# First pairs' loads and transposes rearranged, a written-out end, and the last chunk's rows as two halves, in a top-k attention and gated layer kernel

## The chip, the cores and the metric

The kernel runs on one core of one Trainium2 chip. The metric is the device time of that core in microseconds (us); of several executions the median counts.

## The reference

```python
scores = scale * np.matmul(q, k.transpose(0, 1, 3, 2))          # (8, 8, 576, 576), head size 64
kth = np.partition(scores, -32, axis=-1)[..., -32:-31]
scores = np.where(scores >= kth, scores, -1e9)
attn = softmax(scores)                                           # sum + 1e-09 below
x = np.matmul(attn, v).transpose(0, 2, 1, 3).reshape(4608, 512)
H = np.maximum(x @ w_h, 0.0)
T = 1.0 / (1.0 + np.exp(-(x @ w_t + b_t)))
out = T * H + (1.0 - T) * x
```

Each row of 576 scores keeps its 32 largest, goes through a softmax and is multiplied with v; the 4608 rows of 512 then pass a gated layer with two 512 x 512 weights.

## The kernel before, in words

**Tiling.** Of the 576 query rows of a head, four chunks have 128 rows and the last has 64. A unit is one full chunk of one head, or the last chunk of two heads (64 rows each, so 128 partitions). Two units make a pair; a batch has 18 pairs (four for each full chunk, two for the last chunk) and the run has 144, numbered 0 to 143. k and q are loaded with rows on partitions (`kin`, `qin`, one buffer each) and turned by TensorE (PE) into `kT` and `qT` by `prep_piece` (L210): part 0 turns k of a head pair, part 1 q, part 2 the 64 end rows of all heads.

**A step.** `step(i)` (L641) works on several pairs at once. For pair i+2 PE computes the scores (`start_scores`, L590); for pair i+1 VectorE (DVE) takes twelve MAX8 over segments of the scores in PSUM (`segs`, L603, with the MAX8 at L319), refines them to a threshold (`refine`, L324), ScalarE (ACT) copies the scores to SBUF (L314) and makes the masks (`masks_of`, L636); for pair i PE adds the masks into PSUM (`mask_add`, L373), DVE takes two MAX8 over 576 columns (`below`, L385), ACT takes the exponentials (L382) and the k-th value is picked (`hits`, `pick_a`, `pick_b`); for pair i-1 DVE masks the exponentials (`keep`, L428, or `keep_min` and `keep_mul`), and SyncE (SP) issues a DMA transpose (L447); for pair i-3 PE multiplies with v (`values`, L450) and ACT copies the sums out when four heads are in the bank (`back_xs`, L622). `spare(n)` (L240) issues n matmuls whose result is not used; their moving operand is the weight `wh`.

**The gated layer.** When a chunk's eight heads are there, `ffn_pieces` (L479) makes its pieces: `norm`, `xt` (PE turns x), `hh` and `tt` (the two products, through one PSUM bank, `fps`), each in a step of its own; their sums and products are single operations in the list `pool_work`, which GpSimd (POOL) works off, and the last of them stores the rows. The last chunk goes through this with 64 partitions and 512 columns.

**Start.** POOL sets the constants (L90 to L150), then issues the ten loads of v and the two of the weights (L174 to L203); SP issues the twenty loads of k and q of batch 0 (L158, L164). The code at L735 to L743 then does pair 0 by hand; `ensure_prep` (L575) turns the head pair that a score needs and has ACT copy it, one piece after the other, through the one `fps` bank.

**End.** L744 runs `step` three times more than there are pairs, so the last three steps hold only what is left; then a count over all thresholds makes a flag (L752 to L767), and L770 to L778 works off the rest of the gated layer, one piece at a time, with DVE in POOL's place. The flag decides whether a general second pass runs (L781); it does not run here.

The order on each engine is the order of this code (`manual_schedule`, L734).

Of the kernel before, what the change touches and what calls it, by code (L numbers as in the profile page):

```python
# [26 lines left out]
def kernel(  # L27
# [50 lines left out]
    xpool = ctx.enter_context(tc.tile_pool(name="x", bufs=2))  # L78
# [9 lines left out]
    nc.vector.tensor_copy(ident_b[:], ident_f[:])  # L88
    cst = consts.tile([P, P], BF16)
    nc.gpsimd.memset(cst[:], 1.0 / float(P))  # L90
    ones = consts.tile([P, 1], FP32)
    nc.gpsimd.memset(ones[:], 1.0)
    NPK = TOP_K - RANK + 1
    pidx = consts.tile([P, NPK], FP32)
    for jj in range(NPK):
        nc.gpsimd.memset(pidx[:, jj : jj + 1], S - 2.0 * (TOP_K - jj))
# [3 lines left out]
    nc.gpsimd.memset(fac[:, 0:2], -scale)  # L100
    nc.gpsimd.memset(fac[:, 2:4], -BIGK * (1.0 - 2.0**-24))
# [4 lines left out]
    for i in range(NE):  # L106
        en = consts.tile([P, 2, 2, 16], FP32, name=f"en{i}")
        nc.gpsimd.memset(en[:, 0, :, 0:1], 3.0e38)
        ends.append(en)
# [18 lines left out]
    for i in range(NM):  # L128
        m1 = consts.tile([P, S], BF16, name=f"m{i}")
        nc.gpsimd.memset(m1[:], 0.0)  # L130
        masks.append(m1)

    vbs = []
    for i in range(2):
        vb = consts.tile([P, H, nck, DE], BF16, name=f"vb{i}")
        nc.gpsimd.memset(vb[:], 1.0)
        vbs.append(vb)
    NEP = 4
    eps_sb = []
    for i in range(NEP):  # L140
        ep = consts.tile([P, SP], BF16, name=f"ep{i}")
        pad = S if i % 2 == 0 else 0
        nc.gpsimd.memset(ep[:, pad : pad + SP - S], 0.0)
# [10 lines left out]
    def loads_kq(b, kin, qin):  # L154
        both = ((k, kin), (q, qin))

        def head(src, dst, h):
            nc.sync.dma_start(  # L158
# [4 lines left out]
        def ends(src, dst, i):  # L163
            nc.sync.dma_start(  # L164
                dst[0:rem, :, J, i, :], src[b, i:H:2, J * P : S, :].rearrange("h p d -> p h d")
            )
# [26 lines left out]
    for load in loads_kq(0, kin, qin):  # L193
# [6 lines left out]
    for load in loads_v(0, vbs[0]):  # L200
        load()
    nc.gpsimd.dma_start(wh[:], moe_w_h.rearrange("(g p) n -> p g n", p=P))
    nc.gpsimd.dma_start(wt[:], moe_w_t.rearrange("(g p) n -> p g n", p=P))  # L203
    nc.scalar.dma_start(
        bt32[:], bass.AP(tensor=moe_b_t.tensor, offset=moe_b_t.offset, ap=[[0, P], [1, dm]])
    )
    nc.gpsimd.tensor_scalar_mul(bt[:], bt32[:], 0.5)


    def prep_piece(stage, prep, hp, part):  # L210
# [6 lines left out]
        ps = fps.tile([P, 512], FP32, tag="fp", name="fp")  # L217
        if part < 2:
# [3 lines left out]
            return lambda: nc.scalar.copy(dst[:, hp, 0 : nfull * P], ps[:, 0 : nfull * P])  # L222
# [7 lines left out]
        view = ps[:].rearrange("p (i h n) -> p i h n", i=2, n=rem)  # L230

        def evac():
            nc.scalar.copy(kd[0:D, :, 0:rem], view[0:D, 0, :, :])
            nc.scalar.copy(kd[D:P, :, rem : 2 * rem], view[D:P, 0, :, :])
# [5 lines left out]
    def spare(n):  # L240
        if "t" not in po:
            po.update(t=pso_tile(), n=0)
        for _ in range(n):
# [3 lines left out]
                wh[:, 0, 0 : BANK - 4 * DE],  # L247
# [201 lines left out]

    def values(pair, ets, vb, pso, col):  # L450
        for s, u in enumerate(pair):
            b, qt, heads = units[u]
            ql = rem if qt == nfull else P
            for gi, h in enumerate(heads):
                for c in range(nck):
                    vc = (c - s) % nck
                    nc.tensor.matmul(  # L457
                        pso[0:ql, col : col + DE],
# [11 lines left out]
    def xs_copy(qt, h0, n, pso, xs):  # L470
        ql = rem if qt == nfull else P
        nc.scalar.copy(xs[0:ql, h0 * DE : h0 * DE + n], pso[0:ql, 0:n])  # L472
# [5 lines left out]

    def ffn_pieces(b, qt, xs):  # L479
        ql = rem if qt == nfull else P  # L480
        st = {}

        def norm():
            xs3 = xs[0:ql, :].rearrange("p (h e) -> p h e", e=DE)
            rinv = cpool.tile([P, H], FP32, name="rinv")
            nc.vector.tensor_scalar(rinv[0:ql, :], xs3[:, :, D], 1e-9, 2.0, ALU.add, ALU.mult)
            nc.vector.reciprocal(rinv[0:ql, :], rinv[0:ql, :])
# [3 lines left out]
            def scaled(e):  # L491
                e.tensor_tensor(
                    x[0:ql, :].rearrange("p (h d) -> p h d", h=H),
                    xs3[:, :, 0:D],
                    rinv[0:ql, :].unsqueeze(2).to_broadcast([ql, H, D]),
# [6 lines left out]
        def xt():  # L502
            ps = fps.tile([P, 512], FP32, tag="fp", name="fp")
            for g in range(n_g):
                nc.tensor.transpose(
                    ps[:, g * P : g * P + ql], st["x"][0:ql, g * P : (g + 1) * P], ident_f[0:ql, 0:ql]
                )
# [3 lines left out]
            return lambda: nc.scalar.copy(xT[:, :, 0:ql], psv[:, :, 0:ql])  # L511

        def hh():
            ps = fps.tile([P, 512], FP32, tag="fp", name="fp")
            for g in range(n_g):
                nc.tensor.matmul(
                    ps[0:ql, :], st["xT"][:, g, 0:ql], wh[:, g, :], start=(g == 0), stop=(g == n_g - 1)
                )
# [5 lines left out]
            def evac():  # L524
                nc.scalar.activation(h2[0:ql, :], ps[0:ql, :], AF.Relu)
                pool_work.append(lambda e: e.tensor_add(s1[0:ql, :], h2[0:ql, :], x[0:ql, :]))
                pool_work.append(lambda e: e.tensor_sub(h2[0:ql, :], h2[0:ql, :], x[0:ql, :]))
# [3 lines left out]
        def tt():  # L531
            ps = fps.tile([P, 512], FP32, tag="fp", name="fp")
            for g in range(n_g):
                nc.tensor.matmul(  # L534
                    ps[0:ql, :], st["xT"][:, g, 0:ql], wt[:, g, :], start=(g == 0), stop=False
                )
            nc.tensor.matmul(ps[0:ql, :], cst[:, 0:ql], bt[:], start=False, stop=True)
# [3 lines left out]
            def last(e):  # L541
                o = fpool.tile([P, dm], FP32, name="o")
                e.tensor_add(o[0:ql, :], s1[0:ql, :], h2[0:ql, :])
                r0, r1, rs = (qt, J * P, J) if qt < nfull else (J * P, S, 1)
                if isinstance(b, int):
                    dst = out3[b, r0:r1:rs, :]
                else:
# [319 lines left out]
```

## Time and profile before

| | us |
|---|---|
| median of 3 runs | 855.37 (854.66 to 858.37) |
| profiled execution | 860.02 |
| its span, first to last instruction | 858.4 |
| DVE busy | 808.2 (94%) |
| ACT busy | 777.6 (91%) |
| PE busy | 728.8 (85%) |
| POOL busy | 522.2 (61%) |

Busy time is the time in which an engine executes an instruction; PE's is modelled, since matmuls overlap. [...] A line of the timeline tells its start, its length, the engine, the line of the code, what it wrote and read, how many alike follow each other, and in brackets how long the engine had been idle and whom it waited for.

### The profile page before, as it was taken

Reading aid. Unit: us, or ns where it says so; the run is one execution under the profiler, and the core shown is the slowest. Engines: PE = TensorE matmul, PEld = TensorE weight load, DVE = VectorE, ACT = ScalarE, POOL = GpSimd, SP = SyncE. Lnnn points to the kernel's source line nnn. Section 1 sums busy time; section 2 is a strip of 40 time slices with the busy share of each in tenths; the row PEclk is TensorE's granted clock in tenths of the full one; section 3 lists DMA queues with packets and bytes.
Section 4 is the critical chain, followed back from the end, with each engine's and each line's share of the span. In section 5 each row is a group of like instructions: output and inputs, shape, how many; then the busy total and the mean of one; then the engine's idle time right before and its main releaser. Section 6 shows DMA issues by size and latency. Waiting matters only on the chain.

```text
span 858.4 us, 20956 instructions
## 1 busy us (share of the span) xinstructions
PE 728.8 (85%) x6548; PEld 525.1 (61%) x6644; DVE 808.2 (94%) x4131; ACT 777.6 (91%) x1441; POOL 522.2 (61%) x690
## 2 busy tenths in 40 slices
PE   4788988889888888899888998888888998888874
PEld 3566766666566666566666665666665666665652
DVE  5599999999999999999999999999999999999973
ACT  3589998999999999999999999999999999999961
POOL 9145655766657566666656666576666666555560
PEclk9699999999999999999999999999999999999997
DMA  9466545666367545664555754576445644442331
GB/s 158 72 105 110 95 67 115 118 117 91 73 110 132 98 81 94 115 125 85 78 110 121 123 88 76 105 134 101 81 92 116 124 82 82 80 86 62 81 75 35
DMA packets 318631, 83.52 MB, mean 97 GB/s; under 512 B 312752, under 2 KB 313776, under 8 KB 318512
## 3 DMA queue, kind: packets, MB, share of 16 engines
q1 hardware_dynamic: 275072, 75.55, 42.9%
q0 software_dynamic: 43296, 6.30, 10.6%
q8 instruction: 54, 0.88, 0.4%
q14 instruction: 65, 0.53, 0.2%
q10 hardware_dynamic: 144, 0.26, 0.2%
HBM read 31.72 MB, written 9.44 MB: 48 GB/s over the span
## 4 chain that ended last, share of the span: by engine, by line
ACT 38%; PE 32%; DVE 25%; POOL 2%; issue 2%; DMA 1%; ACTq 0%; POOLq 0%; DVEq 0%
ACT m L363 10%; DVE wall L386 9%; DVE cand L319 9%; ACT e L382 9%; PE pso L244 8%; ACT sc L314 6%; PE xs L275 6%; ACT r L409 4%; PE xs L292 3%; PE pso L457 3%; PE fp L534 3%; PE xs L376 3%; ACT xs L472 2%; PE xs L284 2%; ACT kT L222 2%
## 5 line engine op out<-in xcount | busy, mean ns | idle before, releaser
L319 DVE MAX8 cand<-xs 128x8 f32<-128x96 f32 x1728 | 297.0, 247 | 22.2 <-PE xs L284 16.9
L244 PE MATMUL pso<-wh,ident_b 128*128 128x252 bf16 x1962 | 261.2, 273 | 47.7 <-ACT xs L472 45.5
L244 PEld LDWEIGHTS <-ident_b 128*128 128x128 bf16 x1962 | 186.5, 98 | 91.1 <-issue 59.6
L382 ACT ACTIVATE e<-sc,be 128x576 bf16<-128x576 f32 x288 | 228.2, 793 | 0.2 <-POOL be L357 0.2
L386 DVE MAX8 wall<-xs 128x8 f32<-128x576 f32 x288 | 203.8, 749 | 7.7 <-PE xs L376 4.2
L275 PE MATMUL xs<-kT,qT 64*128 64x256 f32 x1024 | 148.6, 406 | 37.8 <-DVE high L333 30.8
L314 ACT COPY sc<-xs 128x1152 f32<-128x1152 f32 x144 | 161.6, 1122 | 10.1 <-DVE cand L319 10.1
L420 POOL TENSOR_SCALAR ro<-sc,tk 128x576 bf16<-128x576 f32 x93 | 160.0, 1721 | 0.0
L275 PEld LDWEIGHTS xs<-kT,qT 64*128 64x128 f32 x1024 | 94.8, 189 | 67.5 <-issue 34.8
L402 POOL TENSOR_TENSOR hit<-hit,wall 128x18 f32<-128x18 f32 x144 | 32.6, 226 | 151.0 <-DVE hit L392 139.1
L363 ACT ACTIVATE m<-xs,wall 128x576 int8<-128x576 f32 x144 | 107.8, 749 | 15.9 <-DVE wall L349 15.7
L357 POOL TENSOR_TENSOR be<-tk,fac 128x4 f32<-128x4 f32 x145 | 28.8, 198 | 150.9 <-DVE ep L426 48.8
L409 ACT ACTIVATE r<-sc,be 128x576 bf16<-128x576 f32 x144 | 112.2, 779 | 1.9 <-POOL be L357 1.9
L363 ACT ACTIVATE m<-sc,wall 128x576 int8<-128x576 f32 x144 | 112.8, 783 | 0.0
L376 PE MATMUL xs<-m,ident_b 128*128 128x64 bf16 (+1 forms) x520 | 94.3, 277 | 10.6 <-ACT m L363 8.8
L457 PEld LDWEIGHTS <-et 128*128 128x128 bf16 (+1 forms) x1600 | 68.6, 100 | 18.9 <-issue 3.7
L457 PE MATMUL pso<-vb,et 128*128 128x65 bf16 (+1 forms) x1600 | 74.4, 194 | 3.6
L376 PEld LDWEIGHTS <-ident_b 128*128 128x128 bf16 x576 | 51.8, 98 | 38.7 <-issue 14.6
L284 PEld LDWEIGHTS xs<-kd,qT 128*128 128x128 f32 x256 | 38.7, 190 | 43.4 <-issue 43.4
L416 DVE TENSOR_TENSOR ep<-e,r 128x576 bf16<-128x576 bf16 x144 | 65.1, 452 | 0.0
L284 PE MATMUL xs<-kd,qT 128*128 128x128 f32 x256 | 63.4, 330 | 0.0
L174 POOL DMA_DIRECT2D vb<-in_v_dram x64 | 52.1, 815 | 7.1 <-issue 7.0
(87 smaller groups left out, 1184.0 us busy)
## 6 DMA issues: line engine op xcount, KB each, us to landing
kin<-in_k_dram SPq DMA_DIRECT2D x64, 128.0 KB, 2.6
qin<-in_q_dram SPq DMA_DIRECT2D x64, 128.0 KB, 3.1
out_dram<-o SPq DMA_DIRECT2D x32, 256.0 KB, 2.4
vb<-in_v_dram POOLq DMA_DIRECT2D x80, 64.0 KB, 3.1
et<-ep SPq DMA_TRANSPOSE x288, 2.5
kin<-in_k_dram SPq DMA_DIRECT2D x16, 64.0 KB, 2.5
qin<-in_q_dram SPq DMA_DIRECT2D x16, 64.0 KB, 2.4
out_dram<-o SPq DMA_DIRECT2D x8, 128.0 KB, 2.3
```

The source lines that it names most:

```text
L244: nc.tensor.matmul(po["t"][:, 4 * DE : BANK], ident_b[:], wh[:, 0, 0 : BANK - 4 * DE], start=True, stop=True, skip_group_check=True,)
L275: nc.tensor.matmul(ps[:, mo + n0 : mo + n0 + 256], qT[r : r + D, hp, qs : qs + P], kT[r : r + D, hp, n0 : n0 + 256], start=(n0 == 0), stop ...
L284: nc.tensor.matmul(ends, qT[:, hp, qs : qs + P], kd[:, hp, :], start=True, stop=True)
L314: nc.scalar.copy(sc[:], both)
L319: nc.vector.max(cand[:, s, :], sc[:, s * SEG : (s + 1) * SEG])
L363: nc.scalar.activation(m1[:].bitcast(I8)[:, 1 : 2 * S : 2], ps, AF.Sign, bias=wall[:, u, 0:1], scale=ABOVE, accum_out=csum[:, u : u + 1],)
L376: nc.tensor.matmul(ps[:, s0:s1], ident_b[:], m1[:, s0:s1], start=False, stop=True, skip_group_check=True)
L382: nc.scalar.activation(e[:], sc, AF.Exp, bias=tb(u), scale=scale)
L386: nc.vector.max(wall[:, u, 1:NPK], ps)
L409: nc.scalar.activation(r[:], sc, AF.Relu, bias=eb(u), scale=BIGK)
L420: nc.gpsimd.tensor_scalar(r[:], sc, kth(u), None, ALU.is_ge)
L457: nc.tensor.matmul(pso[0:ql, col : col + DE], ets[s][:, c, gi * P2 : gi * P2 + ql], vb[:, h, vc, :], start=(c == 0), stop=(c == nck - 1),)
```

## The change

Three parts. **Start:** the constants that POOL set go to DVE for the most part; both identities are made by POOL; of `vb` only the column of ones is set. The first q loads are issued by ACT, those of k by SP, the bias by SP at the end. The loads of v and of the weights (in four halves) come out of the start and are issued by POOL in steps 0 to 8, two in each of the steps 0 to 4, then one. `begin()` takes the place of the code at L735: 24 spare matmuls first, with the constant `cst` as moving operand in place of `wh`; then the three pieces of head pair 0 into three PSUM tiles, evacuated by ACT and DVE; the pieces of head pairs 1 and 2 go out ahead of their scores, and pair 3's in steps 0 and 1. **Last chunk as two halves:** its sums of heads 0 to 3 go to partitions 0 to 63, those of heads 4 to 7 to partitions 64 to 127, in one bank with one copy; the gated layer works on 128 partitions and 256 columns, with two groups of matmuls for each product and two stores. **End:** the loop stops after step 142, and `finish()` writes the rest out: all masks by the one-instruction form `keep` on DVE, the last pair's exponentials turned by PE instead of by DMA, the layer's three last blocks (z, ya, yb) in several PSUM banks with fused DVE operations (`blk_diff`, `blk_out`), and the count for the flag last.

```diff
-    nc.vector.tensor_copy(ident_b[:], ident_f[:])
+    make_identity(nc, ident_b[:])
-        nc.gpsimd.memset(vb[:], 1.0)
+        nc.gpsimd.memset(vb[:, :, :, D:DE], 1.0)
-    for load in loads_kq(0, kin, qin):
+    first, later = (loads_kq(0, kin, qin, eng) for eng in (nc.scalar, nc.sync))
+    early = first[0:12] + later[12:]
+    for load in early[0:8]:
         load()
-    for load in loads_v(0, vbs[0]):
-        load()
...
-                wh[:, 0, 0 : BANK - 4 * DE],
+                cst[:, 0 : BANK - 4 * DE],
...
+    def project(ps, qt, xT, w, bias):
...
+        nh, ng, wd = shape_of(qt)
+        for c in range(2):
+            o = ps[c * P2 : (c + 1) * P2, 0:wd]
+            cols = slice(c * wd, (c + 1) * wd)
+            for g in range(n_g):
+                r = g // ng * P2
+                nc.tensor.matmul(
+                    o, xT[:, g % ng, r : r + P2], w[:, g, cols], start=(g == 0), stop=(g == n_g - 1 and not bias)
+                )
...
-        if todo_v and k_in % 3 != 0:
+        for _ in range(min(len(todo_v), 2 if i < 5 else i <= SPB or k_in % 3 != 0)):
             todo_v.pop(0)()
+        if i == 4:
+            nc.gpsimd.tensor_scalar_mul(bt[:], bt32[:], 0.5)
...
+    def begin():
...
+        spare(24)
+        evs = [
+            piece(0, 0),
+            piece(0, 1, po["t"], dve),
+            piece(0, 2, xps.tile([P, 3 * BANK], FP32, tag="x", name="xs"), dve),
+        ]
+        po.clear()
+        for ev in evs:
+            ev()
         start_scores(0)
+        evs = [piece(1, 0), piece(1, 1, pso_tile())]
+        for ev in evs:
+            ev()
         segs(0, 2 * NSEG)
         copy_both(0)
         start_scores(1)
...
+        evs = [piece(2, 0), piece(2, 1, pso_tile())]
         masks_of(0)
+        for ev in evs:
+            ev()
+        to_prep.extend(((0, 3, 0), (0, 3, 1)))
...
+    def finish():
...
+        z = blocks[-1]
+        values_of(i - 3, 0)
+        for s in range(2):
+            mask_add(cur["ps"][s], cur["m"][s], s)
+        late.pop(0)()
+        zh = fps.tile([P, 512], FP32, tag="fp", name="fp")
+        project(zh, z["qt"], z["xT"], wh, False)
+        for s in range(2):
+            ep, last = masked(pu, s, old)
+            old["et"][s] = transposes(ep)
...
+        below(pr[0], cur["ps"][0])
+        below(pr[1], cur["ps"][1])
...
+        for s, home in enumerate((bank(x2, 1), bank(x1, 0))):
+            ep, last = masked(pr, s, cur)
+            turned = home.bitcast(BF16)[:, 0:SP]
+            for c in range(nck):
+                nc.tensor.transpose(turned[:, c * P : (c + 1) * P], ep[:, c * P : (c + 1) * P], ident_b[:])
+            nc.scalar.copy(cur["et"][s][:].rearrange("p c q -> p (c q)"), turned)
+        values_of(i - 1, 0)
+        blk_norm(ya)
+        blk_xt(ya, bank(x1, 2))
+        n = values_of(i, 0)
+        yb = xs_of(nfull, 0, n)
+        project(bank(x1, 0), ya["qt"], ya["xT"], wh, False)
+        do_work(nc.vector, len(pool_work))
+        blk_norm(yb)
...
+        blk_diff(z, zh)
+        blk_out(z)
...
+        blk_diff(ya, bank(x1, 0))
+        blk_out(ya)
+        blk_gate(yb, bg)
+        blk_diff(yb, bank(x2, 0))
+        blk_out(yb)
+        flags_a()
+        flags_b(x2)
...
-        for i in range(NG + 3):
-            step(i)
+        begin()
+        for i in range(NG - 1):
+            step(i)
+        finish()
```

## Rows read from the trace of the kernel before

**Rows 1.** The page's first part: busy us, share of the span, instructions.
```profile
PE 728.8 (85%) x6548; PEld 525.1 (61%) x6644; DVE 808.2 (94%) x4131; ACT 777.6 (91%) x1441; POOL 522.2 (61%) x690
```

**Rows 2.** Windows: stretch, its length, busy us of each engine, PEclk, DMA share, GB/s.
```profile
200.00:780.00 580.00, 509.48 (x4660) 367.56 (x4729) 570.90 (x2977) 557.19 (x1039) 368.58 (x472) 1.00 0.55 99
```

**Rows 3.** Timeline, DVE: the twelve MAX8 of pairs 0, 4 and 5.
```profile
13.79 2.08 DVE L319 MAX8 cand<-xs 128x8 f32<-128x96 f32 x12 [3.94 <-PE xs L284]
...
45.77 2.07 DVE L319 MAX8 cand<-xs 128x8 f32<-128x96 f32 x12
...
50.99 2.07 DVE L319 MAX8 cand<-xs 128x8 f32<-128x96 f32 x12
```

**Rows 4.** Chain that ended last, start: start us, us, what.
```profile
15.87 1.35 POOL vb L180 x2
17.22 7.57 DMA wh<-in_moe_w_h_dram
...
24.83 1.84 PE pso L244 x8
```

**Rows 5.** Timeline of the start: constants, first transposes, copy, scores, the bias.
```profile
0.93 0.06 DVE L111 MEMSET tk<- 128x2 f32 x1 [0.93 <-PEq L851]
...
1.57 8.28 DVE L88 CAST ident_b<-ident_f 128x128 bf16<-128x128 f32 x1 [0.54 <-POOL ident_f masks.py:199]
...
6.55 1.08 PE L221 MATMUL fp<-ident_f,kin 128*128 128x128 f32 x4 [6.55 <-DMA kin<-in_k_dram]
...
7.67 0.58 ACT L222 COPY kT<-fp 128x512 f32<-128x512 f32 x1 [5.12 <-PE fp L221]
...
18.74 1.60 POOL L207 TENSOR_SCALAR bt<-bt 128x512 bf16<-128x512 f32 x1
18.95 2.08 PE L275 MATMUL xs<-kT,qT 64*128 64x256 f32 x8 [0.68 <-ACT qT L222]
```

**Rows 6.** Timeline of steps at a granted clock of 1.00.
```profile
36.34 0.60 PE L221 MATMUL fp<-ident_f,kin 128*128 128x128 f32 x4
...
44.09 1.13 PE L275 MATMUL xs<-kT,qT 64*128 64x256 f32 x8 [1.16 <-DVE high L333]
...
45.15 0.74 ACT L363 ACTIVATE m<-xs,wall 128x576 int8<-128x576 f32 x1 [0.65 <-DVE wall L349]
...
45.48 1.24 PE L244 MATMUL pso<-wh,ident_b 128*128 128x252 bf16 x10
...
47.75 1.41 DVE L386 MAX8 wall<-xs 128x8 f32<-128x576 f32 x2
47.98 1.10 ACT L314 COPY sc<-xs 128x1152 f32<-128x1152 f32 x1
...
55.31 0.83 POOL L174 DMA_DIRECT2D vb<-in_v_dram  x1 [0.23 <-issue]
```

**Rows 7.** Windows of 1 us: the granted clock falls, and rises again.
```profile
18.00:19.00 1.00, 0.32 (x5) 0.09 (x3) 0.00 (x0) 0.69 (x2) 1.00 (x3) 0.62 1.80 208
...
35.00:36.00 1.00, 0.94 (x8) 0.73 (x8) 0.25 (x1) 1.00 (x1) 0.00 (x0) 0.84 0.00 0
```

**Rows 8.** Timeline of the end, from the last pair's twelve MAX8 on.
```profile
818.49 2.08 DVE L319 MAX8 cand<-xs 128x8 f32<-128x96 f32 x12 [0.45 <-PE xs L301]
...
825.68 1.43 DVE L386 MAX8 wall<-xs 128x8 f32<-128x576 f32 x2 [1.68 <-PE xs L376]
...
828.41 0.81 DVE L431 SCALAR_TENSOR_TENSOR ep<-sc,tk,e 128x576 bf16<-128x576 f32 x1
...
831.11 1.84 PE L244 MATMUL pso<-wh,ident_b 128*128 128x252 bf16 x8 [2.75 <-ACT xs L472]
...
834.99 0.83 PE L457 MATMUL pso<-vb,et 128*64 128x65 bf16 x20
...
837.73 0.69 DVE L543 TENSOR_TENSOR o<-s,h 128x512 f32<-128x512 f32 x1 [3.33 <-POOL h L553]
...
843.29 1.02 PE L534 MATMUL fp<-wt,xT 128*128 128x512 bf16 x4 [0.74 <-ACT h L525]
...
850.31 0.59 ACT L552 ACTIVATE tt<-fp 64x512 f32<-64x512 f32 x1 [2.44 <-PE fp L537]
...
852.36 0.50 SPq L549 DMA_DIRECT2D out_dram<-o  x1
```

More of the change, by code (lines that the diff above doesn't have):

```diff
@@ L448, in transposes, with row_of @@
         return et
+    def row_of(pair):
+        return P2 if units[pair[0]][1] == nfull and units[pair[0]][2][0] else 0
     def values(pair, ets, vb, pso, col):
@@ L452, in values @@
             b, qt, heads = units[u]
-            ql = rem if qt == nfull else P
+            r0, ql = row_of(pair), rem if qt == nfull else P
             for gi, h in enumerate(heads):
@@ L479, in ffn_pieces, with store @@
+    def store(b, qt, o):
+        rows = out3[b] if isinstance(b, int) else out3[bass.ds(b, 1)].rearrange("o s n -> (o s) n")
+        if qt < nfull:
+            nc.sync.dma_start(rows[qt : J * P : J, :], o[:])
+            return
+        wd = dm // 2
+        for c in range(2):
+            nc.sync.dma_start(rows[J * P : S, c * wd : (c + 1) * wd], o[c * P2 : (c + 1) * P2, 0:wd])
+    blocks = []
     def ffn_pieces(b, qt, xs):
-        ql = rem if qt == nfull else P
-        st = {}
+        nh, ng, w = shape_of(qt)
+        st = dict(b=b, qt=qt, xs=xs)
+        blocks.append(st)
@@ L532, in tt @@
             ps = fps.tile([P, 512], FP32, tag="fp", name="fp")
[L533 to L537, printed above, removed]
+            project(ps, qt, st["xT"], wt, True)
             t = fpool.tile([P, dm], FP32, name="tt")
@@ L617, in back_pv @@
         if not po["n"]:
-            po["h"] = heads[0]
-        po["n"] = values(pairs[g], st[g]["et"], vbs[b % 2], po["t"], po["n"])
-        po["full"] = po["n"] == 4 * DE
+            po["h"] = heads[0] if qt < nfull else 0
+        po["n"] = values(pairs[g], st[g]["et"], vbs[b % 2], po["t"], po["n"] if qt < nfull else 0)
+        po["full"] = po["n"] == 4 * DE and (qt < nfull or row_of(pairs[g]) > 0)
     def back_xs(g):
@@ L732, in step @@
             todo_kq.pop(0)()
-    with tc.manual_schedule():
+    def begin():
+        done.update((0, hp, part) for hp in range(3) for part in range(2))
+        done.add((0, 0, 2))
+        piece = partial(prep_piece, stages[0], preps[0])
+        dve = nc.vector.tensor_copy
+        spare(24)
[7 more added lines that the diff above has]
+            ev()
         start_scores(0)
+        evs = [piece(1, 0), piece(1, 1, pso_tile())]
+        for ev in evs:
+            ev()
         segs(0, 2 * NSEG)
@@ L780 @@
+    with tc.manual_schedule():
+        for load in early[8:] + [load_bt]:
+            load()
+        begin()
+        for i in range(NG - 1):
+            step(i)
+        finish()
     bad = nc.values_load(flag[0:1, 0:1], min_val=0, max_val=1)
```

242 lines of the change are left out of this document (159 added, 83 removed).

## The prediction

> **What bounds the kernel now.** I read the page's busy shares first, then the windows, then the chain of waits at both ends, then the timeline there. DVE leads with 94% [rows 1], and the windows show that this mean hides two kinds of stage: from 200 to 780 us DVE is busy 570.90 of 580 us [rows 2], so the middle is bound by DVE and by nothing else, while the missing time sits at the two ends. How much: in the middle a pair takes 50.99 - 45.77 = 5.22 us [rows 3]. Pair 0's twelve MAX8 start at 13.79 and pair 4's at 45.77 [rows 3], four pairs in 32.0 us where 20.9 would do; and 13.79 us go by before the first. At the other end the last pair's MAX8 start at 818.49 and the span ends at 858.4, 39.9 us later [rows 8]. About 13.8 + 11.1 + 39.9 = 65 us are start and end; the change works there.
>
> At the start the chain runs through POOL's constants and the v loads to the load of wh (7.57 us), which the eight spare matmuls at 24.83 wait for [rows 4]. Beside that, transposes and copies follow one another through one bank, and PE runs at the low level: four transposes take 1.08 us and eight score matmuls 2.08 us [rows 5] against 0.60 and 1.13 [rows 6]. The granted clock falls in the window from 18 us, after PE had stood idle but for one group of transposes, and rises in the one from 35 us, after PE had gone from one matmul to the next for some time [rows 7]. At the end the layer's pieces follow one another through one bank, with waits of 1.68, 2.75, 3.33 and 2.44 us on different engines [rows 8].
>
> **The change part by part: start.** The spare matmuls need only the two constants, ready at about 1.9 us (POOL's identities; DVE's memsets are short: one takes 0.06 us beside POOL's [rows 5]). A spare costs 1.84 / 8 = 0.23 us at the low level [rows 4] and 1.24 / 10 = 0.124 us at the high one [rows 6]; 24 of them end between 1.9 + 3.0 = 4.9 and 1.9 + 5.5 = 7.4 us. k's second head is SP's second load, no longer its third, so the first transposes can't start before about 6.55 - 0.67 = 5.9 us [rows 5]. I take 6.9 us, nearer the slow end since PE starts cold. From there at the high level: three pieces of 0.60 us back to back [rows 6]; DVE's copy of q ends 2.0 us after the first transpose (no row has DVE copying; I take ACT's 0.58 [rows 5] and add 0.1, and its end is 0.75, by MAX8's 1.41 / 2 [rows 6]); scores 1.13 [rows 6] plus about 0.45 for the end columns: the first MAX8 start 3.55 us after the first transpose, at 10.45 us instead of 13.79.
>
> From that point (call it C) I walk the queues. DVE: MAX8 C to C+2.1, refine to C+3.45. PE meanwhile turns head pair 1 and, after ACT's two copies, computes pair 1's scores until C+3.5, so DVE goes on at once. ACT then carries the masks of pair 0 (two of 0.74) and two more copies of 0.58, and DVE's two MAX8 of 1.41 end at C+7.0; pair 2's scores wait for that bank and end at C+8.65. In step 1 ACT becomes the late one: relu, exponential, 1.10 for the scores' copy, 0.58 for head pair 3, so pair 3's scores end at C+15.75 and DVE waits 1.5 us. Pair 4's MAX8 start at C+21.3 = 31.8 us against 45.77, **14.0 us** earlier.
>
> What is moved costs this. POOL issues two v loads in each of steps 0 to 4, 0.83 us each [rows 6], ahead of the biases; behind them on POOL stand the bias product and POOL's mask for the next step, and ACT's relu waits for the bias. In the middle ACT has 0.65 us of slack before the masks [rows 6]; the second load takes about that, nothing is lost. In step 4 the bias of the gate (1.60 us [rows 5]) comes on top: about 0.7 us once; if that cover is gone, 1.6. The ACT queue issues six loads ahead of its first copy, but these are done by about 5 us. SP's first load of batch 1 waits for head pair 3's turn, as before, and the DMA transposes behind it are not ready earlier. Start: 14.0 - 0.7 = **13.3 us**. Bounds: at the low level throughout, each of the first four pairs costs 1.0 more for scores, and 18 spares 18 x 0.106 = 1.9: 4 x 2.9 = 11.6, so the gain is between 1.7 and about 14.6 (24 spares at the high level).
>
> DVE's cast stood 8.28 us while POOL worked [rows 5]; were the new memsets held up the same way until POOL's shorter list ends at about 4 us, the spares would start 2 us later and the gain be 11.3. [...]
>
> **Last chunk.** Seven times in the middle (batch 7's is in the end part): one ACT copy fewer, POOL's operations half as wide, but 18 matmuls with 256 columns instead of 9 with 512, and one store more on SP. All this lies beside DVE, which is busy 570.90 of 580 [rows 2] and gets no instruction more or fewer. I take 0. No row shows products in two halves; the nearest is the product of 1.02 us for four [rows 8]: were the halves twice that, 2 x 1.0 us a batch would fall on PE, whose slack per step is (580 - 509.48) / 580 x 5.22 = 0.63 us [rows 2], so 0.8 a batch at most, 5 us in all; below nothing, DVE's rest of 9.1 us [rows 2] caps a gain, and little of it is the layer's: 0 to -1.
>
> **End.** Up to the masks of pair 143 nothing changes; its MAX8 start at 825.68 as before [rows 8]. In the wait of 1.68 us ahead of them DVE now does pair 142's two `keep` (0.81 [rows 8], 0.74 apart). After 827.1: hit and pick 0.4, two `keep` to 829.0. The DMA transpose goes; five PE transposes (0.5) and an ACT copy of 640 columns (between 0.58 [rows 5] and 1.10 [rows 6]; 0.7, as 512 columns are nearer) have the second one at 830.45. Behind it on PE: `values` of pair 142 (0.83 [rows 8]), ya's turn (0.60), `values` of pair 143 (0.83): 831.9; copy, 832.25. The DVE work of the block before (two of 0.69) and ya's norm lie in that wait. From there DVE is the chain: yb's norm 0.75, then z and ya with three operations of about 0.73 each (0.69 [rows 8] to 0.81), yb with three of 0.4: 832.25 + 0.75 + 4.4 + 1.2 = 838.6, where the last store is issued, against 852.36 [rows 8]: 13.7 us. PE's last product ends at 837.0, just ahead of its use. What follows the store (858.4 - 852.36 = 6.0 us) stays; the flag's 2.6 us now come after the last store but beside its landing. About 15 handoffs that I drew too tight cost about 1 us: **12.7 us**. Bounds: with PE at the low level, six products of about 1 us take twice that, -6; if the handoffs cost nothing, +1.
>
> **Sum.** 13.3 + 12.7 = 26.0; I take 1 off for what two hand-drawn walks leave out: 25. Profiled: 860.0 - 25 = 835.0. The profiled execution lies 860.02 - 855.37 = 4.65 above the median, so the median becomes 855.4 - 25 = **830.4**.
>
> **Rivals.** *The clock stays low at the start* (or falls in steps 0 to 3, when PE waits for ACT's copies). For it: the fall at 18 us after a pause [rows 7], the slow spares after the wait of 2.75 us at the end [rows 8], and `begin` has no spare matmuls between the pieces. Against it: 24 spares first, and no pause of PE above 1.5 us in my walk. It takes 10 us off the gain: 840.4. *The end is serial after all*: PE's order holds each product behind `values` and turns that wait for ACT; products at the low level, 6 us: 836.4. *The v loads on POOL count*: 0.83 us in each of steps 0 to 8, as ACT's slack is used up there, 7.5 us: 837.9. *It does not do what it says*: the memsets are held (2 us) and the first pieces still go one after the other (two copies of 0.58 and their handoffs, twice, 3 us): 835.4. *Slower*: PE's clock does not hold in the first steps and the kernel stays at the low level for many. At low level PE's 4.6 us a step [rows 2] become up to 8 or so, 2.8 over DVE's 5.22: from about (25 + 4.3) / 2.8 = 10 such steps on it is slower; twenty would give 830.4 + 56 = 886. Against it: in the kernel before, spares in each step brought the clock up in the third step and kept it [rows 7].
>
> **How the numbers follow.** Forecast 0.62 (826 to 834); clock at the start 0.13; serial end 0.10; loads 0.05; not as said 0.06; slower 0.04. Range: the upper bounds of both ends (14.6 and 13.7) and of the middle (1) give 29.3, so 826; up to the clock case gives 841. A measurement of this kernel tells about 0.5% from no change, 4.3 us. All cases but the last lie more than that below 855.4; the clock case with the serial end would leave 846, and part of the unforeseen reaches no change: faster 0.92, same 0.04, slower 0.04.
>
> **What would show it.** Right: first MAX8 near 10.5 us, pair 4's near 32; granted clock 1.00 from about 7 us on; DVE 5.22 us a pair in the middle; from the last twelve MAX8 to the last store 20 us instead of 34; DVE nearly without a pause in the last 6 us. Wrong: score groups of 2 us after 10 us; ACT waiting for the bias in steps 1 to 8; PE waiting for DVE's copies; a pair in the middle that is not 5.22 us.

## The result, and the profile after

The changed kernel takes **833.48 us** (median of 4 runs, 832.52 to 834.34); the kernel before, on the same chip, 856.66 us (4 runs, 854.66 to 858.37). The ratio is 0.973, with a 95% interval of 0.9702 to 0.9758. Forecast were 830.4 us with 826 to 841, and faster with a chance of 0.92: the time lies 3 us above the forecast and inside the range. The profiled execution took 834.34 us with a span of 832.7 us, 25.7 us less than the 858.4 us of before; forecast were 25.

The page's first part, after (the columns of [rows 1]), and the windows from 200 to 780 us (those of [rows 2]):

```profile
PE 715.4 (86%) x6674; PEld 517.8 (62%) x6674; DVE 801.1 (96%) x4161; ACT 769.9 (92%) x1428; POOL 490.1 (59%) x660
```
```profile
200.00:780.00 580.00, 508.88 (x4762) 367.64 (x4763) 571.77 (x2995) 554.93 (x1034) 352.93 (x472) 1.00 0.55 99
```

DVE is still the busiest engine, at 96% of a shorter span. In the middle it is busy 571.77 of 580 us against 570.90 [rows 2]: it loses a little less there, and the same window holds 18 more of its instructions.

The best ruler for this kernel is the start of each pair's twelve MAX8, in both traces. The timeline of DVE after, for pairs 0, 3 and 4:

```profile
10.42 2.07 DVE L329 MAX8 cand<-xs 128x8 f32<-128x96 f32 x12 [0.91 <-PE xs L294]
...
25.10 2.07 DVE L329 MAX8 cand<-xs 128x8 f32<-128x96 f32 x12 [0.44 <-PE xs L294]
30.33 2.06 DVE L329 MAX8 cand<-xs 128x8 f32<-128x96 f32 x12
```

Pair 0 starts 13.79 - 10.42 = 3.37 us earlier than in [rows 3], pair 4 45.77 - 30.33 = 15.44. This distance, followed through all pairs, says where the time went. (One execution's start is sure to about 0.8 us: in the eight traces of this text that have this start with all its spare matmuls, the distance at pair 4 lies between 15.1 and 16.0.)

| stretch | how the distance goes | worth, us | forecast, us |
|---|---|---|---|
| start, to pair 4 | 0 to 15.44 | 15.4 | 14.0 |
| pairs 7 to 10 | 15.44 to 14.88 | -0.6 | -0.7 |
| middle, to pair 143 | 14.88 to 17.49, in small steps | 2.6 | 0 |
| last twelve MAX8 to the last store's issue | 33.87 us, now 20.60 | 13.3 | 13.7 |
| last store's issue to the end of the span | 6.0 us, now 11.1 | -5.1 | 0 |
| handoffs and what the walks leave out | | in the rows above | -2 |
| sum | | 25.7 | 25 |

So the span's total came out by luck: two misses, 2.6 us in the middle and 1.4 at the start, with the 2 us held back for what the walks leave out, about made up for a third, 5.1 us behind the last store. (That the median still lies 3 us above the forecast has another reason, told below.) The experiments are about these.

**The start.** The timeline after (those lines of it that answer to [rows 4] and [rows 5]):

```profile
1.53 1.22 DVE L130 MEMSET m<- 128x288 uint32 x4
...
1.84 4.93 PE L254 MATMUL pso<-cst,ident_b 128*128 128x252 bf16 x24 [1.84 <-POOL ident_b masks.py:199]
...
6.75 0.63 PE L231 MATMUL fp<-ident_f,kin 128*128 128x128 f32 x4
6.90 1.28 ACT L232 ACT_TABLE_LOAD   x1 [6.90 <-DMA qin<-in_q_dram]
...
8.19 0.58 ACT L232 COPY kT<-fp 128x512 f32<-128x512 f32 x1
...
8.83 1.13 PE L285 MATMUL xs<-kT,qT 64*128 64x256 f32 x8 [0.24 <-ACT kT L232]
```

The spares begin at 1.84 us, once POOL's identity is there; DVE's memsets, four in 1.22 us, are not in the way. The first transposes take 0.63 us instead of 1.08 and the scores 1.13 instead of 2.08 [rows 5]. The copy of kT starts only at 8.19, some 0.8 us after its transposes, since ACT is late. The chain that ended last says why (columns as in [rows 4]):

```profile
1.56 4.71 DMA qin<-in_q_dram
...
6.30 0.57 ACTq L158
```

Six issues of about 0.6 us each would be done by 5 us. But the sixth of ACT's loads waits until the second has landed, at 6.28; it goes out at 6.30, the table load of 1.28 us follows at 6.90, then the copy. So ACT's queue sets the scores' start here, by 0.2 us: DVE's copy of q, behind the spares and the transposes, had ended at 8.54.

**The end.** The timeline after, from the last pair's twelve MAX8 on (it answers to [rows 8]):

```profile
801.00 2.07 DVE L329 MAX8 cand<-xs 128x8 f32<-128x96 f32 x12 [0.45 <-PE xs L311]
...
808.18 1.43 DVE L396 MAX8 wall<-xs 128x8 f32<-128x576 f32 x2 [0.22 <-ACT xT L556]
...
811.56 1.42 ACT L921 COPY et<-xs 128x640 bf16<-128x640 bf16 x2 [0.39 <-PE xs L920]
...
813.75 0.83 PE L470 MATMUL pso<-vb,et 128*64 128x65 bf16 x20
...
815.03 0.17 DVE L598 TENSOR_SCALAR rinv<-xs 128x4 f32<-128x4 f32 x1 [0.91 <-ACT xs L484]
...
821.60 1.12 SPq L521 DMA_DIRECT2D out_dram<-o  x2
...
823.65 0.14 DVE L865 TENSOR_SCALAR flag<-xs 1x1 int32<-1x1 f32 x1 [0.28 <-PE xs L864]
```

The waits of 1.68, 2.75, 3.33 and 2.44 us of [rows 8] are gone; DVE's largest one is 0.91 us. Behind the last store a stretch of 11.1 us is left, of which DVE's count for the flag fills the first 2.2.

### The profile page after: what moved, and what is told of

Its sections match the earlier page's. It is cut to its first block, busy times and chain, and to the rows that moved or that the text cites. A ratio compares the mean times of both kernels' runs of the same rounds, so it can differ in the third digit from the quotient of the medians.

```text
span 832.7 us, 21124 instructions
## 1 busy us (share of the span) xinstructions
PE 715.4 (86%) x6674; PEld 517.8 (62%) x6674; DVE 801.1 (96%) x4161; ACT 769.9 (92%) x1428; POOL 490.1 (59%) x660
## 4 chain that ended last, share of the span: by engine, by line
ACT 39%; DVE 36%; PE 22%; issue 1%; DMA 1%; ACTq 0%; DVEq 0%
DVE cand L329 13%; DVE wall L396 12%; ACT m L373 11%; ACT e L392 9%; ACT sc L324 7%; PE pso L254 4%; ACT r L419 4%; PE xs L285 4%; PE xs L302 4%; PE fp L498 3%; PE xs L386 2%; DVE ep L426 2%; ACT kT L232 2%; ACT xs L484 2%; PE xs L294 1%
## 5 line engine op out<-in xcount | busy, mean ns | idle before, releaser
L254 PE MATMUL pso<-cst,ident_b 128*128 128x252 bf16 x1926 | 256.1, 272 | 41.4 <-ACT xs L484 39.0
L254 PEld LDWEIGHTS <-ident_b 128*128 128x128 bf16 x1926 | 183.0, 98 | 80.5 <-issue 48.5
L285 PE MATMUL xs<-kT,qT 64*128 64x256 f32 x1024 | 145.6, 400 | 42.5 <-DVE high L343 31.8
L430 POOL TENSOR_SCALAR ro<-sc,tk 128x576 bf16<-128x576 f32 x92 | 158.3, 1720 | 0.0
L285 PEld LDWEIGHTS xs<-kT,qT 64*128 64x128 f32 x1024 | 93.5, 186 | 72.4 <-issue 39.9
L386 PE MATMUL xs<-m,ident_b 128*128 128x512 bf16 (+1 forms) x576 | 105.5, 285 | 13.7 <-ACT m L373 11.1
L386 PEld LDWEIGHTS <-ident_b 128*128 128x128 bf16 x576 | 51.5, 97 | 42.6 <-issue 20.5
L174 POOL DMA_DIRECT2D vb<-in_v_dram x64 | 52.3, 818 | 12.0 <-issue 11.1
```

Of the source, the lines that this page charges most:

```text
L254: nc.tensor.matmul(po["t"][:, 4 * DE : BANK], ident_b[:], cst[:, 0 : BANK - 4 * DE], start=True, stop=True, skip_group_check=True,)
L285: nc.tensor.matmul(ps[:, mo + n0 : mo + n0 + 256], qT[r : r + D, hp, qs : qs + P], kT[r : r + D, hp, n0 : n0 + 256], start=(n0 == 0), stop ...
L386: nc.tensor.matmul(ps[:, s0:s1], ident_b[:], m1[:, s0:s1], start=False, stop=True, skip_group_check=True)
L430: nc.gpsimd.tensor_scalar(r[:], sc, kth(u), None, ALU.is_ge)
```

## The experiments

**The flag ahead of the last stores.** What comes behind the last store was the largest miss. In the changed kernel the count and the flag move ahead of `ya`'s output:

```diff
         project(bg, yb["qt"], yb["xT"], wt, True)
+        flags_a()
+        flags_b(bank(x1, 2))
         blk_diff(ya, bank(x1, 0))
...
         blk_out(yb)
-        flags_a()
-        flags_b(x2)
```

> The changed kernel with the count for the flag moved ahead of the outputs of ya and yb. Theory (the branch): after the flag is read, PE's branch takes 4.8 us and all engines wait for it; 4 us earlier it lies beside the outputs. The last store is issued 2.3 us later (the count's DVE work), and the span ends about 6.6 us after it instead of 11.1: span 832.7 + 2.3 - 4.5 = 830.5. Rival (the two last stores hold the end): the 11.1 us behind the first of them stay, span 835.0.

Measured: 833.01 us in one run, span 831.4. That time alone tells nothing, as executions of the change as it is took 832.49 to 834.34; the stretches do. From pair 143's twelve MAX8 (801.43) to the end it took 29.97 us instead of 31.70: 1.7 us gained against that execution, although DVE's 2.3 us of counting now stand ahead of the last stores. (Pair 143 itself came 0.43 later, so that 834.34 - 833.01 = 1.3 us are left in the time. In a second execution of the change as it is, below, the stretch was 30.32, so that the gain lies between 0.35 and 1.7.) The view by source line shows the branch that waits for the flag (columns: the line, the engine's queue, the instruction, how many; shortest, median and longest in ns; first and last start in us). EVENT_SEMAPHORE is what an engine executes first behind its branch. After:

```profile
L955 SPq EVENT_SEMAPHORE  x8: 17/17/17, 829.7 to 830.2; - x8
...
L955 PEldq COMPARE_BRANCH  x1: 4782/4782/4782, 824.6 to 824.6; - x1
L955 SPq COMPARE_BRANCH  x1: 58/58/58, 824.7 to 824.7; - x1
...
L955 DVEq EVENT_SEMAPHORE  x1: 21/21/21, 829.6 to 829.6; - x1
```

The flag early, with the timeline's line of its last two stores:

```profile
L955 PEldq COMPARE_BRANCH  x1: 4938/4938/4938, 821.6 to 821.6; - x1
...
L955 SPq COMPARE_BRANCH  x1: 58/58/58, 825.9 to 825.9; - x1
```
```profile
824.23 1.62 SPq L521 DMA_DIRECT2D out_dram<-o  x2
```

And before, where the flag had been ready early (POOL branches on it at 839.1):

```profile
L781 PEldq COMPARE_BRANCH  x1: 3722/3722/3722, 848.5 to 848.5; - x1
...
L781 SPq COMPARE_BRANCH  x1: 58/58/58, 852.9 to 852.9; - x1
```

Two things read out of these lines. First, SP branches once it has issued the last store *and* the flag can be read: before and with the flag early at once behind the store (852.9 and 825.9), after only at 824.7, 2.0 us behind it. From SP's branch to the end are 858.4 - 852.9 = 5.5 us before and 831.4 - 825.9 = 5.5 with the flag early, but 832.7 - 824.7 = 8.0 after. Second, behind the flag the engines stand still. TensorE's branch takes 3.7 to 4.9 us. The branches of the others take under 0.1, but in the changed kernel ACT, DVE and SP, which branch at 824.4, 824.4 and 824.7, execute their next instruction only at 829.2, 829.6 and 829.7, some 5 us later as well. Before and with the flag early TensorE's standstill lies beside the last stores (its branch ends by the time SP branches, or 0.7 us behind); after all of them lie behind. It is not the stores that are waited for: the last one lands 2.0 us after its issue at 822.1 (median of the two, by the view of the DMA issues), ahead of SP's branch.

**A shorter branch.** To see whether this is the cause of the rest, and where it comes from, the code that the branch jumps over was cut, for all engines: of the second pass, which does not run, only the first pair of a batch is kept, and its gated layer never comes.

```diff
-            for pr in pairs[0 : NG // B]:
+            for pr in pairs[0:1]:
```

> The changed kernel with a shorter second pass: in the branch that is not entered, the loop over a batch's 18 pairs holds only the first pair and no gated layer, so that far fewer TensorE instructions stand between the branch and its target; all work that runs is the same. Theory (TensorE's branch is long because its target lies far ahead in its instructions): TensorE's compare-and-branch takes under 0.2 us instead of 3.6 to 4.8, the engines join about 0.5 us after the flag, and the end is then set by what follows the last store as before (6.0 to 7.2 us after its issue, instead of 11.1 and 9.7): the span is 1.5 to 3 us shorter than the change's 831.2 to 832.7, and the median lies near 831. Rival (the branch's length is TensorE's own, from waiting for or emptying its queue, whatever stands behind it): 3.6 to 5.3 us again, and no difference in the span beyond 0.7 us. [...]

Measured: 831.43 us (median of 4 runs, 830.97 to 831.97), span 830.2, ratio to before 0.9685 (0.965 to 0.972). The change as it is was run again (833.04 us, 5 runs, 832.49 to 833.93; span 831.2), so by the medians the cut gives 1.6 us, without touching anything that runs. The two were not timed side by side, and their ratios to the kernel before (0.9694, 0.9681 to 0.9707, for the change) don't tell them apart; the traces do: from pair 143's twelve MAX8 to the end it takes 29.0 us, against 31.7 and 30.3. The branches:

```profile
L955 SPq EVENT_SEMAPHORE  x8: 17/17/17, 827.7 to 828.2; - x8
...
L955 SPq COMPARE_BRANCH  x1: 54/54/54, 824.6 to 824.6; - x1
...
L955 PEldq COMPARE_BRANCH  x1: 358/358/358, 824.7 to 824.7; - x1
...
L955 DVEq EVENT_SEMAPHORE  x1: 21/21/21, 824.9 to 824.9; - x1
```

TensorE's branch falls from 4782 ns to 358, ACT and DVE go on after 0.5 and 0.2 us, and from SP's branch to the end it is 830.2 - 824.6 = 5.6 us again, as before. The rival, a length of TensorE's own, is out: only the code jumped over is shorter here. The expectation was off in two sizes: the branch takes 0.36 us, not under 0.2, and 8.35 us from the last store's issue to the end remain, not 6.0 to 7.2, because the flag is still late and SP stands still even so, for 827.7 - 824.6 = 3.1 us. In that second execution of the change TensorE's branch took 3618 ns, and from SP's branch to the end it was 831.2 - 824.6 = 6.6 us.

It would be wrong to read TensorE's branch as the link that ends last. In the changed kernel TensorE comes to the closing lines of the program (L1040) at 829.6, SP at 830.3, and SP is through with its own of them at 831.0: SP is last, here as with the short pass. So the 5.1 us of the profiled execution divide into 2.5 us behind SP's branch (8.0 against 5.5) and 2.6 us by which SP branches later behind the last store's issue (824.7 - 821.60 = 3.1 against 0.5; 0.6 of this is the second store's issue). Of the 2.5 us, 1.8 are SP's own standstill (829.7 - 824.7 = 5.0 us; before 856.1 - 852.9 = 3.2, in which the last store also landed). TensorE's branch and SP's standstill differ together between the two executions: 4.8 and 5.0 us, against 3.6 and 3.8 in the second. Whether the standstills lengthen each other was not tried, as no run cut the code of one engine alone; nor why SP keeps its 3.1 us.

In the traces of the kernel before, of the change (two) and of four of its variants, all with the full pass, ACT, DVE, POOL and SP take 45 to 76 ns for the branch and TensorE 3558 to 5282. Why TensorE's is long over a long piece of code was not shown. The view of the DMA queues has queues of the kind "instruction": from 824 to 827 us of the changed kernel they move these packets (packets, MB, share), and none from 815 to 825:

```profile
q8 instruction: 2, 0.03, 7.6%
q14 instruction: 4, 0.03, 3.3%
```

For which engine a packet is, and whether a branch waits for it, no row tells.

**No spare matmuls at the start.**

```diff
-        spare(24)
+        spare(0)
```

> The changed kernel without the 24 spare matmuls at the start. Theory (they buy the clock): first transposes near 5.9 us, when k lands, but at the low level, so transposes of 1.1 us a group and scores of 2.1 us; first MAX8 near 11.5 us instead of 10.4, each of the next pairs 1 us later still, pair 4's near 34 instead of 30.3, span 836 or more. Rival (they only delay, since the clock rises anyway with the work): first MAX8 near 9.6, pair 4's near 29.5, span 832.

Measured: span 833.4. The timeline of the start without the spares, and one window of 1 us (columns as in [rows 7]):

```profile
6.69 1.09 PE L231 MATMUL fp<-ident_f,kin 128*128 128x128 f32 x4 [6.69 <-DMA kin<-in_k_dram]
...
9.50 1.49 PE L285 MATMUL xs<-kT,qT 64*128 64x256 f32 x8
...
11.25 0.60 PE L231 MATMUL fp<-ident_f,kin 128*128 128x128 f32 x4
...
11.45 2.08 DVE L329 MAX8 cand<-xs 128x8 f32<-128x96 f32 x12 [0.86 <-PE xs L294]
```
```profile
7.00:8.00 1.00, 1.00 (x7) 1.00 (x6) 0.00 (x0) 1.00 (x1) 0.00 (x0) 1.00 0.80 147
```

The first MAX8 start at 11.45 instead of 10.42, and this 1.0 us stays constant (pair 4 at 31.38). The theory's first half, 11.5, is right; its second, another 1 us for each pair, is wrong, and so is the rival's 9.6: after the low level's 1.09 us the scores fall on the change of level (1.49, between 1.13 and 2.08 of [rows 6] and [rows 5]), and the next transposes take the high level's 0.60. Two more readings. k lands at 6.69 here, and the spares of the changed kernel end at 6.77, so they cost next to nothing. And the windows' column of TensorE's granted clock (PEclk) shows 1.00 at 7 us although the transposes take the time of the low level: this early, the level is read from durations, and the prediction's sign of a clock of 1.00 from about 7 us on could not have told anything. The 1.0 us is of one execution against another; against all eight with the spares, whose first MAX8 start between 9.90 and 10.72, it is 0.7 to 1.6.

**The new start alone**, in the kernel before: the constants, loads and `begin()` of the change, and nothing of the other two parts.

```diff
+        spare(24)
+        evs = [
+            piece(0, 0),
+            piece(0, 1, po["t"], dve),
+            piece(0, 2, xps.tile([P, 3 * BANK], FP32, tag="x", name="xs"), dve),
+        ]
...
         start_scores(0)
+        evs = [piece(1, 0), piece(1, 1, pso_tile())]
...
         for i in range(NG + 3):
             step(i)
```

> The kernel before with the new start alone (loads, constants, begin, v and weights in the steps). Theory (the three parts add up): first MAX8 at 10.4 us, pair 4's at 30.3, some 0.6 us lost again in pairs 7 to 10, then the same distance of 14.9 us to the kernel before up to the end: span 843.5, median 841.8. Rival (part of the start's gain needs the narrower layer of the last chunk): the distance changes over the batches and ends below 13.

Measured: 844.82 us (843.27 to 846.33, 4 runs) against 859.97 (854.5 to 860.49, 7 runs), ratio 0.9837 (0.9794 to 0.988). The distance is 3.07 at pair 0, 15.13 at pair 4, 14.56 at pair 10 and then stays between 14.1 and 14.7 up to pair 143 (14.64). The theory holds: the start gives what it gives by pair 10, and the middle takes none of it back. So most of the 2.6 us gained in the middle of the changed kernel come from another part. (At the end 0.9 us are lost again, 40.7 us behind pair 143 instead of 39.9: span 844.6, expected 843.5.)

**The last chunk's halves alone**, in the kernel before: `project` and `row_of` of the change, the copy of the sums, the pieces on 128 partitions and 256 columns, two stores.

```diff
-                nc.scalar.activation(h2[0:ql, :], ps[0:ql, :], AF.Relu)
+                nc.scalar.activation(h2[:, 0:w], ps[:, 0:w], AF.Relu)
...
-                nc.scalar.activation(t[0:ql, :], ps[0:ql, :], AF.Tanh)
+                nc.scalar.activation(t[:, 0:w], ps[:, 0:w], AF.Tanh)
```

> The kernel before with the last chunk as two halves alone. Theory (narrower operations of ACT let PE and DVE go on sooner): pairs start 0.2 us sooner in two steps of each batch, 0.36 us a batch from batch 1 on and 2.1 to 2.6 us by the last pair; at the end the last block's operations are half as wide, 1.5 to 2 us more: span about 854. Rival (all of it lies beside DVE, as predicted): no change up to the last pair, span 856.5.

Measured: span 854.0. The distance is 1.51 from pair 3 to pair 27 (the start's code is unchanged, so this is not the edit's); then it grows by 0.17 at pair 28, by 0.21 at pair 30, so on in each batch, and is 3.78 at pair 143: 2.3 us won in the middle, where nothing was forecast. Of these, 0.39 come at pair 137 alone, and the kernel with the new start alone gains 0.35 there too: about 1.9 us are the edit's own. That the span came out as expected is luck, since 1.5 us of it are not the edit's. The timeline ahead of pair 28's twelve MAX8 shows how the edit works. Before:

```profile
173.59 0.60 ACT L525 ACTIVATE h<-fp 64x512 f32<-64x512 f32 x1
...
176.95 0.37 ACT L235 COPY qT<-fp 128x256 f32<-128x256 f32 x1
...
176.98 0.45 DVE L426 TENSOR_TENSOR ep<-e,ro 128x576 bf16<-128x576 bf16 x1
177.01 0.49 PE L284 MATMUL xs<-kd,qT 128*128 128x128 f32 x2
...
177.53 2.08 DVE L319 MAX8 cand<-xs 128x8 f32<-128x96 f32 x12
```

With the halves:

```profile
172.10 0.41 ACT L557 ACTIVATE h<-fp 128x256 f32<-128x256 f32 x1
...
175.28 0.37 ACT L235 COPY qT<-fp 128x256 f32<-128x256 f32 x1
...
175.33 0.49 PE L284 MATMUL xs<-kd,qT 128*128 128x128 f32 x2
...
175.86 2.08 DVE L319 MAX8 cand<-xs 128x8 f32<-128x96 f32 x12
```

Relu takes 0.41 us instead of 0.60. Everything behind it on ACT comes earlier by that, among it the copy of the next batch's end columns (3.18 us behind relu's start instead of 3.36); PE's scores wait for this copy, and DVE's MAX8 for the scores: before, DVE's own work ended at 177.43 and the scores at 177.50, and the MAX8 start at 177.53; with the halves the scores are there at 175.82, ahead of the end of DVE's own work, and it goes on without a pause. Pair 28 comes 175.86 - 170.63 = 5.23 us after pair 27 instead of 177.53 - 172.13 = 5.40. In this step of the kernel before ACT, not DVE, is the late one. For pair 30 the same was not followed line by line. At the end the edit gives 39.9 - 39.3 = 0.6 us, less than the 1.5 to 2 expected.

The page of the kernel before could have warned. Its chain that ended last is, by engine:

```profile
ACT 38%; PE 32%; DVE 25%; POOL 2%; issue 2%; DMA 1%; ACTq 0%; POOLq 0%; DVEq 0%
```

**The last pair turned by DMA again**, in the changed kernel:

```diff
-        for s, home in enumerate((bank(x2, 1), bank(x1, 0))):
+        for s in range(2):
             ep, last = masked(pr, s, cur)
-            turned = home.bitcast(BF16)[:, 0:SP]
...
+            cur["et"][s] = transposes(ep)
```

> The changed kernel with the last pair's exponentials turned by two DMA transposes again instead of by PE and ACT. Theory (the turn lies on the path that sets the end): a transpose takes 1.25 us to issue and about 2.5 to land, so the last product with v starts near 0.9 us later and the last store too: from the last pair's MAX8 to the last store 21.5 us instead of 20.6. Rival (hidden: DVE is the chain there anyway): 20.6 as before.

Measured: 835.1 us, span 833.4. Its timeline of the end:

```profile
815.20 0.76 PE L470 MATMUL pso<-vb,et 128*64 128x65 bf16 x10 [0.88 <-DMA et<-ep]
...
816.41 0.17 DVE L598 TENSOR_SCALAR rinv<-xs 128x4 f32<-128x4 f32 x1 [2.54 <-ACT xs L484]
...
823.49 1.12 SPq L521 DMA_DIRECT2D out_dram<-o  x2
```

The last store is issued 823.49 - 800.74 = 22.75 us after the last twelve MAX8 instead of 20.60: PE's turn is worth 2.1 us, more than the 0.9 expected. Pair 142's two turns and pair 143's two go through one queue, issued 1.3 to 1.4 us apart, so the last lands four turns on, and DVE waits 2.54 us for it instead of 0.91.

**The gate's bias one step later**, in the changed kernel, behind POOL's own work of step 5:

```diff
         do_work(nc.gpsimd, min(work, len(pool_work)))
+        if i == 5:
+            nc.gpsimd.tensor_scalar_mul(bt[:], bt32[:], 0.5)
...
-        if i == 4:
-            nc.gpsimd.tensor_scalar_mul(bt[:], bt32[:], 0.5)
```

> The changed kernel with POOL's product for the gate's bias moved from step 4 (behind two v loads, ahead of the biases) to step 5, behind POOL's mask and ahead of pick_a. Theory (ACT's relu waits for the biases behind that product): the 0.56 us that pairs 7 to 10 lose against the kernel before come back, distance 15.4 us at pair 18 instead of 14.9. Rival (the two v loads a step cost it): the loss stays, 14.9.

Measured: span 831.6, 833.21 us. The distance falls from 15.77 at pair 6 to 15.49 at pair 7 and stays there: 0.28 us lost instead of 0.56. After, in the timeline of step 4, the product makes `be` late, and ACT waits for it:

```profile
41.45 1.53 POOL L780 TENSOR_SCALAR bt<-bt 128x512 bf16<-128x512 f32 x1
...
43.19 0.78 ACT L419 ACTIVATE r<-sc,be 128x576 bf16<-128x576 f32 x1 [1.45 <-POOL be L367]
```

With the product moved, `be` is not held up, but a second effect remains, in DVE's refining:

```profile
42.99 1.50 POOL L754 TENSOR_SCALAR bt<-bt 128x512 bf16<-128x512 f32 x1
...
44.06 0.50 DVE L347 TENSOR_SCALAR neg<-high 128x48 f32<-128x48 f32 x1
```

In other steps this `neg` takes 0.18 us; here it ends just behind POOL's product. (In the change as it is it takes 0.49 us too, at 44.40, beside POOL's mask, which the product has made late.) Each of the two slow ones overlaps an operation of POOL's; why they are slow was not shown. DVE's memsets of the start, beside POOL's, were not stretched like the cast of 8.28 us in [rows 5]: four took 1.22 us and ended at 2.75, ahead of POOL's last one at 3.07.

**A better version.** The changed kernel with the bias moved, the flag early, and `z`'s difference in DVE's wait ahead of `yb`'s norm:

```diff
         do_work(nc.vector, len(pool_work))
+        blk_diff(z, zh)
         blk_norm(yb)
...
         blk_gate(ya, bank(x1, 1))
-        blk_diff(z, zh)
         blk_out(z)
```

> The changed kernel with the count for the flag ahead of the outputs of ya and yb, the bias product in step 5 and z's difference taken while DVE waits for yb's sums. Theory: 1.7 us (branch hidden) + 0.5 (bias) + 0.7 (difference in the wait): span 829.8, about 2.9 us under the changed kernel, 0.35%. Rival (run-to-run scatter is larger than that): no difference from the changed kernel timed beside it.

> The changed kernel as it is, timed beside the one with the three moves and the kernel before. Expected ratio to the kernel before 0.972 to 0.975, span 831 to 833.

Measured beside each other, 5 runs each: **831.32 us** (831.04 to 831.45), ratio 0.9671 (0.9658 to 0.9684), against 833.04 (832.49 to 833.93), ratio 0.9694 (0.9681 to 0.9707), for the change as it is. The executions don't overlap: 1.7 us less, 0.2%; expected were 2.9. DVE's wait ahead of `yb`'s norm fell from 0.91 to 0.40 us; of the two profiled executions' 831.2 - 829.6 = 1.6 us, 0.3 are there by pair 143 (800.88 against 800.57), which is the bias, and 1.3 come behind it. The expectation had taken the flag's full 1.7 us, which it gives only against an execution with long standstills behind the branch:

```profile
814.70 0.17 DVE L598 TENSOR_SCALAR rinv<-xs 128x4 f32<-128x4 f32 x1 [0.40 <-ACT xs L484]
...
822.59 1.78 SPq L521 DMA_DIRECT2D out_dram<-o  x2
```

TensorE's branch takes 5.28 us here, but begins at 820.0 and so ends at 825.3, and SP, which branches at 824.4, goes on after 2.6 us. From SP's branch to the end it is 5.2 us, so the shorter second pass would probably add little to this version (this was not run); it is no version to keep anyway, as it leaves out work that the flag may ask for.

## Why the prediction was right, and where it was not

**The step to the median: a term mis-sized by 3.8 us.** The profiled execution was put at 835.0 us and took 834.34. The median was then reached by taking off the same 4.65 us by which the profiled execution of the kernel before lay above its median; after, it lies 834.34 - 833.48 = 0.86 above. That accounts for the whole distance of 3 us between forecast and median. What the profiled execution of before had lost against the others is open, as only its trace was kept; its granted clock was 0.982, that of the changed kernel's 0.994, and two later executions of the kernel before with 0.995 and 0.998 took 855.57 and 854.5 us, five with 0.982 to 0.992 took 859.27 to 860.49. That the clock is the cause was not shown.

**Start, right in its mechanism, 1.4 us too small.** The first MAX8 were put at 10.45 us and came at 10.42, which is luck, as the path there was another. "The ACT queue issues six loads ahead of its first copy, but these are done by about 5 us" failed: the sixth waits for the second's landing, they end at 6.9, and the table load behind them holds the kT copy until 8.19. The transposes at 6.75 (6.9 drawn) and DVE's copy of q at 8.54 (8.9 drawn) came early enough to hide that, and the scores start at 8.83, as drawn. That DVE's new memsets would not be held up beside POOL, on which the 13.3 us rest, was the author's estimate, with the one memset of 0.06 us behind it; measured were four in 1.22 us. From the first MAX8 the walk gave 21.3 us to pair 4; it took 30.33 - 10.42 = 19.9. The walk had DVE wait 1.5 us for pair 3's scores; the row shows 0.44.

**The lower bound of the start was far too low.** "At the low level throughout" 11.6 us were to be lost; without any spare it was 1.0, since the work of the start had brought the level up by 11.25 us (0.60 us for four transposes). The rival of the clock at the start (840.4) would have needed more than missing spares.

**The loads on POOL and the bias: right.** -0.7 forecast, -0.56 measured, of which half is the late `be` that the text named and half is the slow `neg` (0.50 us instead of 0.18), which it did not. The v loads themselves cost nothing that the distances show; the rival of 837.9 is out.

**Middle: 5.22 us is not what a pair takes there.** The prediction read 50.99 - 45.77 off one pair and called it the middle's. From pair 4 to pair 143 it is (818.49 - 45.77) / 139 = 5.56 us on average before and 5.54 after; 5.2 us are the quickest steps, and where DVE has more to do or waits a pair takes up to 6.1. So its sign "a pair in the middle that is not 5.22 us" was there before the change, the slack that it gave PE in a step is a little too small, and the start's "20.9 would do" is no floor: the four pairs took 19.9.

**Last chunk: the step failed.** "All this lies beside DVE" and "by DVE and by nothing else" took the mean of the middle for every step. In the same window [rows 2] ACT was busy 557.19 us of 580, and the page's chain ran through ACT for 38% and through DVE for 25%. There are steps in which ACT ends last, followed for one of them and seen in each batch at the same two pairs, and 0.2 us less on ACT there is 0.2 us less in time; 1.9 us by the experiment, of the 2.6 gained in all, beyond the bound of -1. The bound came from DVE's idle time of 9.1 us between 200 and 780 us and the guess that "little of it is the layer's"; 1.9 us is about a fifth of it.

**End up to the last store: right.** From the last pair's MAX8 over 576 columns to the last store's issue 12.9 us were drawn (825.68 to 838.6) and 821.60 - 808.18 = 13.4 measured; the 0.5 lies within the 1 us held back for handoffs. One link of it, PE's turn, is worth 2.1 us by its experiment; what the several banks and the fused operations give was not tried apart. The serial end (836.4) did not come.

**Behind the last store: the step failed.** "What follows the store (6.0 us) stays; the flag's 2.6 us now come after the last store but beside its landing" cost 5.1 us. The 6.0 us were taken as the landing of a store alone; in the changed kernel the stores have landed by about 824.1 us and the span ends 8.6 us later. The trace of before had the branch in it: it waits for the flag, and TensorE's took 3.7 us there, ended at 852.2 us, just ahead of the last store's issue, and so cost nothing. A flag that is made last puts the standstill behind the branch, SP's above all, behind the last store.

## What to carry to other kernels

What stands last in a program includes the branch behind it: whatever decides a branch over a long piece of code should be ready some 5 us before the last store (TensorE's branch took up to 5.28 us here, SP's next instruction came up to 5.0 us behind its own), and the branch's own lines, with the first instruction behind it on every engine, belong in the sum. A mean busy share of 98% does not tell that an engine is the bound in every step: the page's chain by engine warns of it, and the start of the same instruction in each round, subtracted between two traces, shows the steps where another one is late. And a lower bound for a slow clock should ask how long the work itself would take to bring it up (here by 11.25 us, without a spare matmul).

## What was not expected of the hardware

TensorE's compare-and-branch over the full second pass took 3.6 to 5.3 us, varying between executions of the same kernel (4.78 and 3.62), against 0.36 over the short one. On ACT, DVE and SP the branch itself took 0.05 to 0.08 us, but in the changed kernel their next instruction came 4.8 to 5.2 us behind it; with the short pass 0.5, 0.2 and 3.1. Fp32 transposes and scores alone brought TensorE from the low level (1.09 us for four transposes at 6.69 us) to the high one (0.60 at 11.25), without a spare matmul. A `tensor_scalar` of 128x48 on DVE took 0.50 us instead of 0.18 while POOL ran one of its own.
